# Float64 weights rounded by a 32-bit sum on GpSimd, and all of w_out converted in the first expert

## The chip, the core and the metric

The kernel runs on one core of one Trainium2 chip. The metric is the device time of one execution in microseconds (us). A core has five engines that run at the same time, each through its own instructions in the order in which they were issued: TensorE (PE, matrix products; its weight loads are PEld), VectorE (DVE), ScalarE (ACT), GpSimd (POOL) and SyncE (SP), which here issues most of the DMA transfers. An engine waits on a semaphore where its next instruction needs another engine's result, and everything queued behind that instruction waits as well.

## What is computed

Three steps follow one another. The inputs of the last, `w_in` and `w_out`, are float64, since float32 draws are multiplied by a float64 factor.

```python
# 1. retention: 4 batches x 768 steps, 8 heads of 64
state = gamma * state + einsum('bhd,bhe->bhde', k[t], v[t])
y[t] = scale * einsum('bhd,bhde->bhe', q[t], state)
# 2. x = y as 3072 tokens of 512; 8 experts with room for 384 tokens each
logits = x @ w_gate                 # filled in descending order of the logits,
out[mask_e] = relu(x[mask_e] @ w1[e]) @ w2[e]     # a token goes to one expert
# 3. for every token, with w_in (512 x 2048) and w_out (2048 x 512)
h = x @ w_in
g = maximum(h, 0) + log1p(exp(-abs(h)))
return g @ w_out
```

## The kernel before, in words

**Attention stage.** `Attn.emit` walks over 24 chunks of 128 tokens (4 batches of 6). For chunk j the loop issues the load of `qk` for chunk j+3 and the store of chunk j-2's rows `xs` to DRAM (`xd`), the scores `pA` of chunk j+1 on PE and their masked copy `at` on DVE (L126), the projection `pX` of chunk j-1 (its rows leave through ACT as `xs`, L168, its logits through DVE, L173), the outputs `pY` of chunk j (L138, L142) and the state `pS` (L155). ACT also copies `yT` and `sb` and scales `vh` (L114). POOL scales `qs` (L106, a product of two tiles). Every chunk's PSUM tile has one buffer, so PE's next `pA` waits for `at`, and its next `pX` for `xs` and the logits. After every sixth chunk `R.first_part` runs the first selection step of the routing on DVE.

**Float64 conversion.** Class `Conv` turns float64 words into float32. A piece of 128 x 512 (or 128 x 256) values arrives as pairs of 32-bit words, `raw[:, :, 0]` the low and `raw[:, :, 1]` the high one. `Conv.size` takes the magnitude of the high word on ACT (L240) and its maximum with a smallest value on POOL (L241). The generator `Conv.run` then does the rest on DVE, one instruction to each step; each `yield` ends a step. A `w_in` piece gives two tiles, a rounded part `wih` and a remainder `wil`: six DVE instructions (L255, L257, L260, L266, L268, L270) and a copy on ACT (L262). A `w_out` piece gives one float32 tile with five (L272, L274, L276, L281, L283). `side(j, part)` is called three times in each chunk and brings the generator to `(3 j - 2 + part) * 112 // 69` steps, so that the 16 `w_in` pieces and the first three `w_out` pieces (`kept = 3`) are spread over the attention stage.

**First routing.** `Route.phase` finds the next expert's 384 tokens by counting against thresholds: DVE compares (`G`, L409), PE counts (L416), DVE decides (L466), PE sums (L472), DVE goes on (L476, L456). This runs once before the first expert, with `fill` placing two conversion steps behind a comparison four times (8 steps in all), and once for every further expert, beside the matmuls of the expert before. In the first expert one step of routing follows every group of matmuls, later one follows every second group.

**Experts.** `Ffn.plan` lists groups of matmuls: `m1` and `m2` (x by `w1`, h by `w2`), then `f1` (by `w_in`, L669 to L672) and `f2` (by `w_out`, L767 to L772). A product of float32 is made of three matmuls of split operands (`split_w`: rounded half on ACT, L646, remainder on DVE, L647; `split_act`, `split_g` the same for activations). In the first expert (`i == 0`, from the fourth group on) `Ffn.emit` issues four or three steps of the conversion `F.late` behind every group: 26 pieces of 128 x 256, the other 13 blocks of `w_out`. `split_w` of a `w_out` block first runs the generator until that block is made.

Of the kernel before, what the change touches and what calls it, by code (L numbers as in the profile page):

```python
# [53 lines left out]
class Attn:  # L54
# [166 lines left out]
class Conv:  # L221
    def __init__(self, tc, ctx, W, plan, bufs=3, lead=1):
        self.nc, self.W, self.plan, self.bufs, self.lead = tc.nc, W, plan, bufs, lead
# [13 lines left out]
    def size(self, p):  # L237
        raw = self.raw.pop(p)
        A = self.st.tile([128, self.W], I32, name="cA", bufs=2 * self.lead)
        self.nc.scalar.activation(A.bitcast(FT), raw[:, :, 1].bitcast(FT), AF.Abs)  # L240
        self.nc.gpsimd.tensor_scalar(A.bitcast(FT), A.bitcast(FT), LEAST, None, op0=OP.max)  # L241
        return A, raw[:, :, 0].bitcast(U32), raw[:, :, 1]

    def run(self):
        nc, v, N = self.nc, self.nc.vector, len(self.plan)
        T = lambda name: self.st.tile([128, self.W], I32, name=name, bufs=2)
        self.ahead(0)
        ready = [self.size(q) for q in range(self.lead)]
        for p in range(N):
            self.ahead(p + 1)  # L250
            A, w0, w1 = ready.pop(0)
            X, to = T("cX"), self.plan[p][1]
            if len(to) == 2:
                f = lambda t: t.rearrange("p (a n) -> p a n", a=4)
                v.tensor_scalar(X, A, 3, 0x3ffff000, op0=OP.logical_shift_left, op1=OP.bitwise_and)  # L255
                yield
                v.scalar_tensor_tensor(X, w1, UPPER, X, op0=OP.bitwise_and, op1=OP.bitwise_or)  # L257
                yield
                C = T("cC")
                v.tensor_scalar(C, A, 0x1ff, 3, op0=OP.bitwise_and, op1=OP.logical_shift_left)  # L260
                yield
                nc.scalar.activation(to[0], f(X.bitcast(FT)), AF.Copy)  # L262
                if p + self.lead < N:
                    ready.append(self.size(p + self.lead))
                U = A.bitcast(FT)
                v.scalar_tensor_tensor(U, w0, 2.0 ** -29, C, op0=OP.mult, op1=OP.add)  # L266
                yield
                v.tensor_scalar(C, X, -0x800000, None, op0=OP.bitwise_and)  # L268
                yield
                v.scalar_tensor_tensor(to[1], f(U), 2.0 ** -23, f(C.bitcast(FT)), op0=OP.mult, op1=OP.mult)  # L270
            else:
                v.tensor_scalar(X, A, 3, 0x3fffffff, op0=OP.logical_shift_left, op1=OP.bitwise_and)  # L272
                yield
                v.scalar_tensor_tensor(X, w1, UPPER, X, op0=OP.bitwise_and, op1=OP.bitwise_or)  # L274
                yield
                v.tensor_scalar(A, X, -0x800000, None, op0=OP.bitwise_and)  # L276
                yield
                if p + self.lead < N:
                    ready.append(self.size(p + self.lead))
                e = A.bitcast(FT)  # L280
                v.scalar_tensor_tensor(e, w0, 2.0 ** -52, e, op0=OP.mult, op1=OP.mult)  # L281
                yield
                v.tensor_tensor(to[0], X.bitcast(FT), e, op=OP.add)  # L283
            self.made += 1
            yield

    def step(self, to=None):

        while to is None or self.ops < to:
            self.ops += 1  # L290
            if next(self.gen, self) is self or to is None:
                return
# [11 lines left out]
class Route:  # L304
# [3 lines left out]
    def __init__(self, tc, cp, wp, psum_tile, L, NCH, E):  # L308
        nc = self.nc = tc.nc
        self.tc, self.L, self.N, self.E, self.wp, self.psum_tile = tc, L, NCH, E, wp, psum_tile  # L310
# [6 lines left out]
        for st in (1, 33, 47):  # L317
            self.stc[st] = t([128, 46], FT, f"st{st}")
# [7 lines left out]
        d = t([128, 128], FT, "diff")  # L326
# [8 lines left out]
        r48 = t([48, 24], FT, "r48")  # L335
        it(r48, pattern=[[1, 24]], base=24, channel_multiplier=-1, **imp)
        c48 = t([48, 1], FT, "c48")
# [11 lines left out]
        cid = t([128, N, 2], FT, "cid")  # L349
# [75 lines left out]
    def phase(self, i, slow=True, hum=lambda n: None, fill=lambda l: None):  # L425
# [13 lines left out]
        for l, (J, s1, sh, span) in enumerate(() if last else LEVELS):  # L439
# [9 lines left out]
            for st in (s1, 1):  # L449
# [26 lines left out]
                v.scalar_tensor_tensor(sc[:, :J], ps[:, 64:64 + J], 0.0, self.stc[st][:, :J],  # L476
# [130 lines left out]
class Ffn:  # L607
# [212 lines left out]
    def emit(self):  # L820
# [9 lines left out]
        for n, (fn, i, f, key) in enumerate(G):  # L830
# [6 lines left out]
            if i == 0 and n > 3:  # L837
                for _ in range(4 if n % 3 else 3):
# [66 lines left out]
def model(ctx, tc, qk, kv, w_gate, w1, w2, w_in, w_out, tab, gqt, out, B, H, S):  # L905
# [11 lines left out]
    kept = 3  # L917
    wo = pers.tile([128, kept, 512], FT, name="wo")
    holder = {}
    R = Route(tc, pers, None, lambda: holder["ps"](), L, NCH, E)  # L920
# [24 lines left out]
    wos = [wo[:, f, :] for f in range(kept)] + [wl[:, f, :] for f in range(16 - kept)]  # L945
# [37 lines left out]
```

## Time and profile before

| what | us |
|---|---|
| median of 3 runs (lowest, highest) | 1054.81 (1052.47, 1056.62) |
| the profiled execution, its own time | 1053.3 |
| its span, first to last instruction | 1051.5 |
| PE busy | 995.6 (95%) |
| DVE busy | 685.6 (65%) |
| ACT busy | 565.8 (54%) |
| POOL busy | 135.1 (13%) |

The busy time is the union of an engine's instructions. The shares of the whole span hide that the stages differ: attention takes about the first 134 us, the first routing goes to about 164, the first expert's groups to about 302, and the other seven follow. A rows section below has the stretches that matter.

### The profile page before, as it was taken

How to read it: one execution, taken by the hardware profiler on the slowest of the kernel's cores; microseconds unless marked ns; L12 is line 12 of the kernel's file. 1: busy time of each engine (PE TensorE's matmuls, PEld its weight loads, DVE VectorE, ACT ScalarE, POOL GpSimd, SP SyncE). 2: the span in 40 equal slices, each digit the busy share in tenths (PEclk: the TensorE clock that was granted, in tenths of full speed). 3: DMA queues.
4: the chain of work that ended last, by engine and by line, in shares of the span. 5: the costliest groups of instructions: out<-in, count | busy, mean ns of one | idle time of the engine just before them, and what ended most of it. 6: DMA issues, size and time to landing. Idle time of an engine off the chain costs nothing.

```text
span 1051.5 us, 19105 instructions
## 1 busy us (share of the span) xinstructions
PE 995.6 (95%) x7266; PEld 901.3 (86%) x7266; DVE 685.6 (65%) x1778; ACT 565.8 (54%) x1194; POOL 135.1 (13%) x153
## 2 busy tenths in 40 slices
PE   5998878888899999999999999999999999999997
PEld 5887658877799889999899889888989899999996
DVE  3989977989856756665566566656665744344442
ACT  4877613455544664366536653665356636664654
POOL 3544401212110101010101001100110020001001
PEclk9999999999999999999999999999999999999999
DMA  9999524312241203210231014101410150014000
GB/s 359 399 353 333 195 86 126 123 60 71 81 121 31 61 11 98 84 31 1 85 107 31 2 50 141 31 1 38 124 41 1 41 181 21 1 33 129 1 1 31
DMA packets 40748, 97.55 MB, mean 93 GB/s; under 512 B 5328, under 2 KB 5456, under 8 KB 40656
## 3 DMA queue, kind: packets, MB, share of 16 engines
q1 hardware_dynamic: 36000, 83.12, 23.7%
q0 software_dynamic: 3840, 12.59, 3.5%
q8 instruction: 57, 0.93, 0.4%
q10 hardware_dynamic: 816, 0.63, 0.2%
q14 instruction: 35, 0.29, 0.1%
HBM read 83.73 MB, written 12.58 MB: 92 GB/s over the span
## 4 chain that ended last, share of the span: by engine, by line
PE 68%; issue 13%; DVE 12%; DMA 3%; ACT 2%; POOL 1%; SPq 0%; ACTq 0%; POOLq 0%; DVEq 0%
PE h L669 11%; PE h L672 11%; PE h L670 10%; PE acc L767 7%; PE acc L768 7%; PE acc L772 7%; PE acc L661 3%; PE acc L663 3%; PE acc L662 3%; PE rt L416 2%; DMA kv_t<-in_kv_dram 1%; PE pX L164 1%; DVE wlo L647 1%; DMA rx<-in_moe_w_gate_dram 1%; DVE at L126 1%
## 5 line engine op out<-in xcount | busy, mean ns | idle before, releaser
L733 DVE SCALAR_TENSOR_TENSOR gf<-h,sp 128x384 f32<-128x384 f32 x128 | 71.3, 557 | 187.4 <-ACT sp L731 187.3
L669 PE MATMUL h<-x2h,wih 128*128 128x384 f32 x512 | 176.4, 345 | 2.2 <-DVE xl L657 2.2
L670 PE MATMUL h<-x2h,wil 128*128 128x384 f32 x512 | 173.0, 338 | 0.0
L767 PE MATMUL acc<-whi,gh 128*128 128x512 f32 x384 | 154.2, 402 | 0.0
L768 PE MATMUL acc<-wlo,gh 128*128 128x512 f32 x384 | 152.1, 396 | 0.0
L729 ACT ACTIVATE sp<-h 128x384 f32<-128x384 f32 x128 | 62.6, 489 | 147.1 <-PE h L672 138.6
L672 PE MATMUL h<-x2l,wih 128*128 128x384 f32 x512 | 112.9, 340 | 0.9 <-DVE x2l L657 0.7
L772 PE MATMUL acc<-whi,gl 128*128 128x512 f32 x384 | 111.9, 398 | 1.9 <-DVE gl L747 1.9
L653 ACT ACTIVATE h1h<-h 128x384 fp32r<-128x384 f32 x64 | 31.5, 492 | 146.7 <-PE h L672 109.6
L669 PEld LDWEIGHTS h<-x2h,wih 128*128 128x128 f32 x512 | 96.7, 189 | 8.0 <-DVE xl L657 2.4
L670 PEld LDWEIGHTS h<-x2h,wil 128*128 128x128 f32 x512 | 96.7, 189 | 3.5
L672 PEld LDWEIGHTS h<-x2l,wih 128*128 128x128 f32 x512 | 91.3, 189 | 3.6 <-DVE x2l L657 3.6
L646 ACT ACTIVATE whi<-wraw 128x512 fp32r<-128x512 f32 x128 | 76.7, 624 | 28.7 <-DMA wraw<-in_moe_w_dram 26.9
L780 POOL DMA_INDIRECT out_dram<-rows,ix x24 | 25.2, 1052 | 514.7 <-ACT rows L778 511.3
L647 DVE TENSOR_TENSOR wlo<-wraw,whi 128x512 fp32r<-128x512 f32 x128 | 86.6, 691 | 6.6 <-ACT whi L646 6.6
L772 PEld LDWEIGHTS acc<-whi,gl 128*128 128x128 f32 x384 | 72.4, 189 | 19.9 <-DVE gl L747 2.5
L669 PE MATMUL h<-xh,whi 128*128 128x384 f32 x256 | 88.3, 345 | 0.7 <-ACT xh L656 0.7
L661 PE MATMUL acc<-h1h,whi 128*128 128x384 f32 x256 | 88.4, 345 | 0.0
L670 PE MATMUL h<-xh,wlo 128*128 128x384 f32 x256 | 86.2, 337 | 0.0
L663 PE MATMUL acc<-h1l,whi 128*128 128x384 f32 x256 | 86.2, 337 | 0.0
L662 PE MATMUL acc<-h1h,wlo 128*128 128x384 f32 x256 | 86.2, 337 | 0.0
L767 PEld LDWEIGHTS acc<-whi,gh 128*128 128x128 f32 x384 | 72.7, 189 | 14.3 <-ACT sp L730 2.9
(208 smaller groups left out, 1922.8 us busy)
## 6 DMA issues: line engine op xcount, KB each, us to landing
wraw<-in_moe_w_dram SPq DMA_DIRECT2D x128, 256.0 KB, 2.8
qk_t<-in_qk_dram SPq DMA_DIRECT2D x24, 512.0 KB, 8.8
kv_t<-in_kv_dram SPq DMA_DIRECT2D x24, 512.0 KB, 8.2
raw<-in_moe_w_in_dram SPq DMA_DIRECT2D x16, 512.0 KB, 6.5
raw<-in_moe_w_out_dram SPq DMA_DIRECT2D x26, 256.0 KB, 2.6
xd<-xs SPq DMA_DIRECT2D x24, 256.0 KB, 6.9
raw<-in_moe_w_out_dram SPq DMA_DIRECT2D x3, 512.0 KB, 7.4
gqt<-in_gqt_dram SPq DMA_DIRECT2D x5, 256.0 KB, 8.5
```

Of the source, the lines that this page charges most:

```text
L646: nc.scalar.activation(hi, raw, AF.Copy)
L647: nc.vector.tensor_tensor(lo, raw, hi.bitcast(FT), op=OP.subtract)
L661: nc.tensor.matmul(ps, wh, ah, start=start, stop=False)
L662: nc.tensor.matmul(ps, wl, ah, start=False, stop=False)
L663: nc.tensor.matmul(ps, wh, al, start=False, stop=stop)
L669: mm(ps, wh(d), ah[:, d], start=d == 0, stop=False)
L670: mm(ps, wl(d), ah[:, d], start=False, stop=False)
L672: mm(ps, wh(d), al[:, d], start=False, stop=d == 3)
L733: nc.vector.scalar_tensor_tensor(g, ps, 0.0, a, op0=OP.max, op1=OP.add)
L767: nc.tensor.matmul(ps, gh[:, s], wh, start=f == 0, stop=False)
L768: nc.tensor.matmul(ps, gh[:, s], wl, start=False, stop=False)
L772: nc.tensor.matmul(ps, gl[:, s], wh, start=False, stop=f == 15)
```

## The change

A `w_in` or `w_out` piece is now made from a sum of 32-bit whole numbers. `size` also takes the low word, scaled, into a tile `cB` on ACT, two pieces ahead in the attention stage (one ahead later). DVE puts sign and upper bits into `cB` (one instruction), shifts and masks `cA` (one), and POOL adds the two as int32 (L259), which rounds. For `w_out` the sum is the result. For `w_in` ACT copies the sum to `wih`, and DVE subtracts one piece later (`late`) to give `wil`.

The three `w_out` pieces of the attention stage are gone (`kept = 0`): all 16 blocks, 32 half pieces, belong to the first expert's generator. The pace is 50 steps in place of 112 in attention and one or two steps behind a group of the first expert. `xs` has three buffers instead of two. Constants of `Route` that are needed only at the start move to a pool that ends with the attention stage; `st` shrinks to one column and is read as a broadcast.

```diff
-        xs = self.wk.tile([128, 2, 2, 128], FT, name="xs")
+        xs = self.wk.tile([128, 2, 2, 128], FT, name="xs", bufs=3)
...
+        B = self.st.tile([128, self.W], I32, name="cB", bufs=self.keep[1])
         self.nc.scalar.activation(A.bitcast(FT), raw[:, :, 1].bitcast(FT), AF.Abs)
         self.nc.gpsimd.tensor_scalar(A.bitcast(FT), A.bitcast(FT), LEAST, None, op0=OP.max)
-        return A, raw[:, :, 0].bitcast(U32), raw[:, :, 1]
+        self.nc.scalar.activation(B, raw[:, :, 0].bitcast(U32), AF.Copy, scale=2.0 ** -29)
+        return A, B, raw[:, :, 1]
...
+            v.scalar_tensor_tensor(B, w1, UPPER, B, op0=OP.bitwise_and, op1=OP.bitwise_or)
+            yield
+            v.tensor_scalar(A, A, 3, 0x3fffffff, op0=OP.logical_shift_left, op1=OP.bitwise_and)
+            nc.gpsimd.tensor_tensor(F, A, B, op=OP.add)
+            if p + self.lead < N:
+                ready.append(self.size(p + self.lead))
+            yield
+            if late:
+                v.tensor_tensor(late[1][1], late[0], late[1][0].bitcast(FT), op=OP.subtract)
+                yield
+            late = None
             if len(to) == 2:
...
+                late = F.bitcast(FT).rearrange("p (a n) -> p a n", a=4), to
+                nc.scalar.activation(to[0], late[0], AF.Copy)
             self.made += 1
...
             if i == 0 and n > 3:
-                for _ in range(4 if n % 3 else 3):
+                for _ in range(1 + n % 2):
                     self.late.step()
...
-    kept = 3
+    kept = 0
...
-    cuts += [(rows[f], (wo[:, f],)) for f in range(kept)]
-    cv = Conv(tc, c1, 512, cuts, 5, 2)
+    cv = Conv(tc, c1, 512, cuts, 5, 2, (5, 4))
...
-            cv.step((3 * j - 2 + part) * 112 // 69)
+            cv.step((3 * j - 2 + part) * 50 // 69)
```

On DVE in the attention stage, from one `at` to the next but one. In the kernel before:

```order
L126 TENSOR_TENSOR at<-pA,ctab 128x1024
L260 TENSOR_SCALAR cC<-cA 128x512
L266 SCALAR_TENSOR_TENSOR cA<-raw,cC 128x512
L268 TENSOR_SCALAR cC<-cX 128x512
L173 TENSOR_REDUCE L<-pX 128x8
L270 SCALAR_TENSOR_TENSOR wil<-cA,cC 128x4x128
L255 TENSOR_SCALAR cX<-cA 128x512
L126 TENSOR_TENSOR at<-pA,ctab 128x1024
```

and in the changed kernel:

```order
L126 TENSOR_TENSOR at<-pA,ctab 128x1024
L256 SCALAR_TENSOR_TENSOR cB<-raw,cB 128x512
L258 TENSOR_SCALAR cA<-cA 128x512
L173 TENSOR_REDUCE L<-pX 128x8
L126 TENSOR_TENSOR at<-pA,ctab 128x1024
L264 TENSOR_TENSOR wil<-cA,wih 128x4x128
```

Between two `at` there stood five conversion instructions, and now one or two.

On POOL in the attention stage, where `cA` is the magnitude and `qs` the scaled q of a chunk. Before:

```order
L106 TENSOR_TENSOR qs<-qk_t,gqt 128x512
L241 TENSOR_SCALAR cA<-cA 128x512
L106 TENSOR_TENSOR qs<-qk_t,gqt 128x512
L241 TENSOR_SCALAR cA<-cA 128x512
L106 TENSOR_TENSOR qs<-qk_t,gqt 128x512
```

and in the changed kernel:

```order
L106 TENSOR_TENSOR qs<-qk_t,gqt 128x512
L259 TENSOR_TENSOR cA<-cA,cB 128x512
L242 TENSOR_SCALAR cA<-cA 128x512
L106 TENSOR_TENSOR qs<-qk_t,gqt 128x512
L259 TENSOR_TENSOR cA<-cA,cB 128x512
L242 TENSOR_SCALAR cA<-cA 128x512
```

A sum of two tiles now stands ahead of every maximum, and the next chunk's `qs` behind both.

On DVE in the first expert, around one decision of the routing (`ind`, which PE's next sum reads). Before:

```order
L647 TENSOR_TENSOR wlo<-wraw,whi 128x512
L276 TENSOR_SCALAR cA<-cX 128x256
L281 SCALAR_TENSOR_TENSOR cA<-raw,cA 128x256
L283 TENSOR_TENSOR wol<-cX,cA 128x256
L272 TENSOR_SCALAR cX<-cA 128x256
L466 TENSOR_SCALAR ind<-rt,r_113 128x46
```

and in the changed kernel:

```order
L637 TENSOR_TENSOR wlo<-wraw,whi 128x512
L258 TENSOR_SCALAR cA<-cA 128x256
L256 SCALAR_TENSOR_TENSOR cB<-raw,cB 128x256
L456 TENSOR_SCALAR ind<-rt,r_121 128x46
```

Four conversion instructions stood ahead of `ind`; now two do, and the second needs a `cB` that ACT is told to make just ahead of it.

## Rows read from the trace of the kernel before

**Rows 1.** Busy time in stretches: us, then engines, granted clock, DMA share, GB/s.

```profile
27.00:60.00 33.00, 29.69 (x454) 26.09 (x451) 31.03 (x57) 24.62 (x74) 16.75 (x11) 0.95 0.99 380
27.00:131.00 104.00, 90.69 (x1414) 79.34 (x1412) 98.93 (x180) 77.44 (x228) 49.18 (x33) 0.97 0.86 321
175.00:266.00 91.00, 80.37 (x560) 72.58 (x559) 84.80 (x251) 45.71 (x98) 22.68 (x25) 0.98 0.29 89
414.00:489.00 75.00, 75.00 (x486) 69.50 (x485) 48.02 (x140) 39.65 (x77) 6.06 (x7) 1.00 0.20 61
```

In these rows the engines stand in the order PE, PEld, DVE, ACT, POOL.

**Rows 2.** Chain that ended last: start, us, what; chunks 2, 3 and 23.

```profile
27.06 1.02 PE pY L142 x16
31.36 1.02 PE pY L142 x16
...
130.56 1.05 PE pY L142 x16
```

**Rows 3.** Waits of PE, 27 to 134 us: total us, times, longest.

```profile
PE pX L164 <- DVE L L173: 6.1, 5, 1.8
PE pA L125 <- DVE at L126: 5.0, 3, 2.4
```

**Rows 4.** One line's matmuls, first and last start; first expert, then the third.

```profile
L661 PE MATMUL acc<-h1h,whi x32: 333/337/423, 175.2 to 207.8; 128*128 128x384 f32 x32
L767 PE MATMUL acc<-whi,gh x48: 391/396/632, 220.3 to 300.8; 128*128 128x512 f32 x48
...
L661 PE MATMUL acc<-h1h,whi x32: 334/337/423, 414.1 to 443.5; 128*128 128x384 f32 x32
L767 PE MATMUL acc<-whi,gh x48: 391/396/478, 450.6 to 519.0; 128*128 128x512 f32 x48
```

**Rows 5.** Waits of PE in the first expert, 175 to 292 us.

```profile
PE rt L472 <- DVE ind L466: 7.2, 6, 2.9
PE rt L526 <- DVE tb L523: 2.3, 1, 2.3
```

**Rows 6.** Three lines of DVE: ns min/median/max, first and last start.

```profile
L255 DVE TENSOR_SCALAR cX<-cA x16: 410/421/1539, 19.8 to 114.8; 128x512 int32<-128x512 int32 x16
...
L257 DVE SCALAR_TENSOR_TENSOR cX<-raw,cX x16: 675/692/1726, 20.6 to 115.3; 128x512 int32<-128x512 int32 x16
...
L647 DVE TENSOR_TENSOR wlo<-wraw,whi x128: 671/685/917, 159.7 to 968.6; 128x512 fp32r<-128x512 f32 x128
```

**Rows 7.** The longest L257 and what POOL ran then: start, us.

```profile
57.27 1.27 POOL L106 TENSOR_TENSOR qs<-qk_t,gqt 128x512 f32<-128x512 f32 x1 [0.54 <-DVE wil L270]
...
57.36 1.73 DVE L257 SCALAR_TENSOR_TENSOR cX<-raw,cX 128x512 int32<-128x512 int32 x1
```

**Rows 8.** Groups by shape, start to 330 us: busy us, mean ns, idle before.

```profile
L241 POOL TENSOR_SCALAR cA<-cA 128x512 f32<-128x512 f32 x19 | 30.5, 1608 | 52.4 <-ACT cA L240 51.3 <-PE pS L155 1.1
L106 POOL TENSOR_TENSOR qs<-qk_t,gqt 128x512 f32<-128x512 f32 x20 | 27.3, 1366 | 14.2 <-DMA qk_t<-in_qk_dram 11.2 <-PE pY L138 1.8 <-DVE cC L260 0.6
L241 POOL TENSOR_SCALAR cA<-cA 128x256 f32<-128x256 f32 x26 | 23.6, 909 | 94.6 <-ACT cA L240 94.6
L168 ACT ACTIVATE xs<-pX 128x512 f32<-128x512 f32 x24 | 14.2, 592 | 14.8 <-DMA xd<-xs 6.9 <-PE pX L164 4.3 <-issue 3.3
L274 DVE SCALAR_TENSOR_TENSOR cX<-raw,cX 128x256 int32<-128x256 int32 x26 | 11.3, 434 | 0.6
L240 ACT ACTIVATE cA<-raw 128x512 f32<-128x512 f32 x19 | 12.7, 676 | 0.0
L240 ACT ACTIVATE cA<-raw 128x256 f32<-128x256 f32 x26 | 11.2, 429 | 27.5 <-DVE wol L283 23.5 <-DVE thr L456 3.9
```

**Rows 9.** One group by shape on DVE, 134 to 300 us.

```profile
L272 DVE TENSOR_SCALAR cX<-cA 128x256 int32<-128x256 int32 x26 | 7.4, 286 | 0.0
```

**Rows 10.** DVE in the first routing, start and us.

```profile
142.72 0.24 DVE L469 TENSOR_SCALAR thrA<-jio,zero 128x46 f32<-128x46 f32 x1
...
143.61 0.80 DVE L409 TENSOR_TENSOR G<-kx,thr 128x552 bf16<-128x552 f16 x2
```

More of the change, by code (lines that the diff above doesn't have):

```diff
@@ L221, with __init__ @@
 class Conv:
-    def __init__(self, tc, ctx, W, plan, bufs=3, lead=1):
-        self.nc, self.W, self.plan, self.bufs, self.lead = tc.nc, W, plan, bufs, lead
+    def __init__(self, tc, ctx, W, plan, bufs=3, lead=1, keep=(3, 2)):
+        self.nc, self.W, self.plan, self.bufs, self.lead, self.keep = tc.nc, W, plan, bufs, lead, keep
         self.st = ctx.enter_context(tc.tile_pool(name="cst", bufs=2, side="right"))
@@ L238, in size @@
         raw = self.raw.pop(p)
-        A = self.st.tile([128, self.W], I32, name="cA", bufs=2 * self.lead)
+        A = self.st.tile([128, self.W], I32, name="cA", bufs=self.keep[0])
+        B = self.st.tile([128, self.W], I32, name="cB", bufs=self.keep[1])
         self.nc.scalar.activation(A.bitcast(FT), raw[:, :, 1].bitcast(FT), AF.Abs)
         self.nc.gpsimd.tensor_scalar(A.bitcast(FT), A.bitcast(FT), LEAST, None, op0=OP.max)
-        return A, raw[:, :, 0].bitcast(U32), raw[:, :, 1]
+        self.nc.scalar.activation(B, raw[:, :, 0].bitcast(U32), AF.Copy, scale=2.0 ** -29)
@@ L244, in run @@
+        return A, B, raw[:, :, 1]
     def run(self):
         nc, v, N = self.nc, self.nc.vector, len(self.plan)
-        T = lambda name: self.st.tile([128, self.W], I32, name=name, bufs=2)
         self.ahead(0)
         ready = [self.size(q) for q in range(self.lead)]
+        late = None
         for p in range(N):
             self.ahead(p + 1)
-            A, w0, w1 = ready.pop(0)
-            X, to = T("cX"), self.plan[p][1]
-            if len(to) == 2:
[L254 to L283, printed above, removed]
@@ new lines, in run @@
+            A, B, w1 = ready.pop(0)
+            to = self.plan[p][1]
+            F = to[0].bitcast(I32) if len(to) == 1 else A
+            v.scalar_tensor_tensor(B, w1, UPPER, B, op0=OP.bitwise_and, op1=OP.bitwise_or)
[5 more added lines that the diff above has]
+            yield
@@ L284, in run @@
+            if late:
+                v.tensor_tensor(late[1][1], late[0], late[1][0].bitcast(FT), op=OP.subtract)
+                yield
+            late = None
+            if len(to) == 2:
+                late = F.bitcast(FT).rearrange("p (a n) -> p a n", a=4), to
+                nc.scalar.activation(to[0], late[0], AF.Copy)
             self.made += 1
-            yield
+        if late:
+            v.tensor_tensor(late[1][1], late[0], late[1][0].bitcast(FT), op=OP.subtract)
+        while True:
+            yield self
@@ L290, in step @@
             self.ops += 1
-            if next(self.gen, self) is self or to is None:
+            if next(self.gen) is self or to is None:
                 return
@@ L304, with __init__ @@
 class Route:
-    def __init__(self, tc, cp, wp, psum_tile, L, NCH, E):
+    def __init__(self, tc, cp, tp, wp, psum_tile, L, NCH, E):
         nc = self.nc = tc.nc
+        x = lambda shape, dt, name: tp.tile(shape, dt, name=name)
         self.tc, self.L, self.N, self.E, self.wp, self.psum_tile = tc, L, NCH, E, wp, psum_tile
@@ L334, in __init__ @@
         v.tensor_scalar(self.u48[0:24, 0:24], d[0:24, 0:24], 0.0, None, op0=OP.is_gt)
-        r48 = t([48, 24], FT, "r48")
+        r48 = x([48, 24], FT, "r48")
         it(r48, pattern=[[1, 24]], base=24, channel_multiplier=-1, **imp)
-        c48 = t([48, 1], FT, "c48")
+        c48 = x([48, 1], FT, "c48")
         it(c48, pattern=[[0, 1]], base=0, channel_multiplier=1, **imp)
@@ L925, in model @@
     rows = [w_out[f * 128:(f + 1) * 128] for f in range(16)]
-    cuts += [(rows[f], (wo[:, f],)) for f in range(kept)]
-    cv = Conv(tc, c1, 512, cuts, 5, 2)
+    cv = Conv(tc, c1, 512, cuts, 5, 2, (5, 4))
+    init = c2.enter_context(tc.tile_pool(name="rinit", bufs=1, side="right"))
+    R = Route(tc, pers, init, None, lambda: holder["ps"](), L, NCH, E)
     a = Attn(tc, c2, aps, qk, kv, w_gate, tab, gqt, ident, L, xd, B, H, S)
@@ L944, in model @@
     wl = late.tile([128, 16 - kept, 512], FT, name="wol")
-    wos = [wo[:, f, :] for f in range(kept)] + [wl[:, f, :] for f in range(16 - kept)]
+    wos = [wl[:, f, :] for f in range(16)]
     R.wp = ctx.enter_context(tc.tile_pool(name="rwork", bufs=1, reuse_waits="tile"))
```

10 lines of the change are left out of this document (4 added, 6 removed).

## The prediction

> **What bounds the kernel now.** I read the stretches first, then the chain, then PE's waits in the two stages that the change touches. Over the whole span PE is busy 95%, and the last seven experts leave nothing to win: between 414 and 489 us PE is busy 75.0 of 75 us [rows 1]. The conversion runs in attention and in the first expert, and there the engine that is full is DVE: 98.9 of 104 us between 27 and 131, and 84.8 of 91 between 175 and 266 [rows 1]. In attention the chain shows chunk 2's `pY` at 27.06 and chunk 3's at 31.36, so PE can do a chunk in 4.30 us; from chunk 3 to chunk 23 it took (130.56 - 31.36) / 20 = 4.96 us for each [rows 2]. PE was idle for 104 - 90.7 = 13.3 us of that stretch, and 11.1 us of waits name two DVE instructions, the logits and `at` [rows 1, 3]. DMA is the neighbour: its share was 0.99 at 380 GB/s while loads ran [rows 1]. In the first expert the stretch from the first `m2` matmul to the last `f2` took 300.8 - 175.2 = 125.6 us, and the same groups of the third expert 519.0 - 414.1 = 104.9 us [rows 4]: 20.7 us more for the same products. PE's waits there name DVE too, most of them a decision of the routing (7.2 and 2.3 us) [rows 5].
>
> **Attention, term by term.** DVE loses per `w_in` piece six instructions: three like L255 (median 0.42 us; L260 and L268 have the same shape) and three like L257 (0.69; L266 and L270) [rows 6], 3.33 us. It gets one like L257, one like L255 and a subtraction like L647 (0.69) [rows 6], 1.80 us. That is 16 x 1.53 = 24.5 us less. The three `w_out` pieces go with five instructions each, 2 x 0.42 + 3 x 0.69 = 2.91, or 8.7 us. Together 33.2 us are taken from DVE.
>
> What is added is a POOL sum of two tiles, 16 times, and here the trace has a warning. While POOL ran the product L106 from 57.27 to 58.54, an L257 that started at 57.36 took 1.73 us instead of 0.69, ending 0.55 us after the product [rows 6, 7]: it stood still until POOL was done. Yet POOL was busy for 49.2 of 104 us, much of it with the maximum L241, and the medians of rows 6 lie within 3% of the minima, so most instructions are not held up, and POOL's one-input work seldom holds any [rows 1, 6]. The new sum has no row. The nearest is L106, a product of two 128 x 512 tiles at 1.37 us [rows 8]; a whole-number sum may cost more or less. Its effect on DVE lies between nothing and its full length, 16 x 1.37 = 21.9 us. I take half, 11 us. DVE's load is then 98.9 - 33.2 + 11 = 76.7 in a stretch of some 97 us, and it stops being the bound.
>
> The Trainium skill, "SBUF — State Buffer", section "Who interferes with whom", says that a VectorE instruction with two SBUF inputs and a GpSimd instruction that reads SBUF exclude each other, and that the one that began keeps the shared port to its end. The L257 above agrees; by that rule at its fullest every sum holds DVE for its length, DVE's load in this stretch would be 87.6 us, and the gain there would shrink to some 4 us.
>
> What is late next? ACT: 16 more instructions like L240 (0.68) and three fewer make 8.8 us on top of 77.4, 86.2 of some 97 us [rows 1, 8], tight but below PE. The copy to `wih` now waits for POOL's sum, and behind it in ACT's queue stand `yT`, `sb` and `xs`, for which PE waits; the copy is issued two steps, nearly a chunk, behind the sum, which hides 1.37 us and the 1.61 us of a maximum ahead of it. POOL gets 16 x 1.37 - 3 x 1.61 = 17.1 us, 66.3 of 97, and `qs` stands behind it, two chunks ahead of its use. DMA: a chunk moves 1 MB of `qk` and `kv`, 0.26 of `xs` and, at 50 steps in place of 112, 0.73 of a 0.52 MB piece in place of 0.81; with `gqt` some 1.7 MB, at 380 GB/s 4.45 us [rows 1]. The third `xs` buffer costs nothing and takes away up to 6.9 us in which ACT waited for stores [rows 8].
>
> So PE's floor is 4.30 us per chunk, DMA's 4.45, and I add 0.15 for ACT's load and the bursts of `first_part`: 4.60. That gives 20 x (4.96 - 4.60) = **7 us gained**. The ends: 13 us (the floor, all of PE's idle time) and 2 us lost (ACT held by late sums).
>
> **The first routing.** Each of the four fills had two DVE instructions, and now has an L257-like and an L255-like one of half the size, the same 0.43 + 0.29 us [rows 8, 9]. Behind them POOL runs the sum (1.37 x 909 / 1608 = 0.77 us, by the ratio of the maximum's two sizes [rows 8]) and the next maximum, while DVE comes to `thrA` and `G` [rows 10], on the path of the decision. Each fill may lose nothing or up to 0.6 us: 0 to 2.4, I take **1 us lost**.
>
> **The first expert.** The 26 half pieces cost 3 x 0.43 + 2 x 0.29 = 1.87 us each [rows 8, 9]; 8 of their 130 steps lie in the routing, so 24.4 x 1.87 = 45.6 us lie here. Now 32 pieces cost 0.72; four lie in the routing, and 28 x 0.72 = 20.2 us here. The 28 sums hold DVE between 0 and 28 x 0.77 = 21.6 us; half is 10.8. Net 45.6 - 20.2 - 10.8 = 14.6 us less on DVE, and 84.8 becomes 70.2, below the 75 us that PE needs for the same groups in the third expert [rows 1]. PE then sets the pace except at the routing's decisions, which still come a group after their count: some of the waits of rows 5 stay. ACT gets 28 x 2 - 24.4 instructions of 0.43 us, 13.6 on top of 45.7 [rows 1, 8], with room. DVE's L256 now waits for `cB`, which in every other piece ACT makes just ahead; two ACT instructions, 0.86 us, against the `h1l` or `gf` and L258 that DVE does meanwhile. SP issues 32 loads of 256 KB in place of 26 here (DMA share 0.29 [rows 1]), and the conversion is always ahead of `until`: it makes 16 pieces by the time the block of `f = 4` needs 10. I take **11 us gained** of the 20.7; the ends are 4 (sums hold DVE to the full) and 17. The remaining experts keep their work.
>
> **Sum.** 7 - 1 + 11 = 17 us, from the profiled execution's 1053.3 to 1036.3. The median of the three runs lies 1.5 us above that execution, so I forecast 1037.5.
>
> **Rivals.** *ACT takes DVE's place in attention.* For it: 86 of 97 us and a copy that waits for POOL. Against: it has nearly a chunk of slack. The gain there is nil: 1053.3 + 1 - 11 = 1043, for the median 1045. *The routing keeps PE waiting in the first expert.* For it: 9.5 us of rows 5 are decisions that follow a chain of PE, DVE and ACT, and DVE now also waits for `cB`; the lock held to the full gives the same. Only 4 us are gained: 1053.3 - 7 + 1 - 4 = 1043, median 1045. *Both stages reach PE's floor.* 13 and 16 us gained, nothing lost: 1024, median 1026. *The whole-number sum is slow, and DVE stands behind it: slower.* It holds DVE to its end; the savings of 33.2 and 25.4 us are used up when a sum takes 33.2 / 16 = 2.1 us in attention and 25.4 / 28 = 0.9 us here. At twice L106 (2.74 and 1.54 us) DVE gets 10.6 and 17.7 us more than before in stages that it bounded: 1053 + 28 = 1081; at one and a half times, with the stages as they were in attention, 32.3 - 25.4 = 7 us more here, 1060. The trace has no whole-number instruction on POOL to say how likely. *It doesn't do what it says*: `until` would have to run the conversion in bursts, which the counts above exclude.
>
> The Trainium skill, "GPSIMD Engine Reference", section "When to use GPSIMD", keeps element by element work on VectorE, since a two-input instruction is about half as fast on GpSimd. Rows 6 and 8 agree (1.37 against 0.69 us); by that rule alone the change would be a loss, which is the slow sum's case and has its chance.
>
> **How the numbers follow.** Forecast 0.46 (1030 to 1041), ACT 0.15, routing 0.18, both at the floor 0.14, slow sum 0.06, not as said 0.01. The predicted time is the likeliest, 1037.5. From 1027 to 1048 the range takes in the forecast, both rivals at 1045 and the upper part of the floor case, and leaves out the rest of it and the slow sum. A measurement tells about 0.5%, 5.3 us, from no change: faster means below 1049.5. All cases but the slow sum and the last lie below, less some spread of those at 1045: faster 0.88, same 0.06, slower 0.06.
>
> **What would show it.** In the changed profile: `pY` of chunk 23 near 123 us; DVE busy some 80% between 27 and the end of attention; PE's waits on the logits and `at` down from 11.1 us to a few; the sum L259 near 1.4 and 0.8 us, and DVE instructions stretched beside it; in the first expert `m2` to the last `f2` about 115 us instead of 125.6. It is wrong if the sum takes over 2 us, if ACT's waits on POOL at the copy to `wih` come to more than a few us, or if PE's waits on `ind` stay at 7 us or grow.

## The result, and the profile after

The changed kernel takes **1038.2 us** (median of four executions, 1036.8 to 1039.7) where the kernel before took 1054.0 in the same session: a ratio of **0.985 (0.982 to 0.988)**. The forecast was 1037.5, within 1027 to 1048. The profiled span fell from 1051.5 to 1037.6 us, 13.9 us less. By stage, from the starts of the same matmuls:

| stage | before | after | difference | forecast |
|---|---|---|---|---|
| start to `pY` of chunk 23 | 130.5 us | 124.8 | -5.7 | -7 |
| to the first `m2` of expert 1 | 44.7 | 47.9 | +3.2 | +1 |
| to the last `f2` of expert 1 | 125.6 | 113.4 | -12.2 | -11 |
| sum | 300.8 | 286.1 | -14.7 | -17 |

These rows answer to rows of before. First the two stretches of [rows 1], engines in the same order:

```profile
27.00:125.00 98.00, 90.92 (x1420) 79.71 (x1418) 69.16 (x123) 82.81 (x239) 63.45 (x45) 0.96 0.86 325
172.00:253.00 81.00, 78.72 (x565) 72.20 (x564) 69.06 (x192) 53.90 (x122) 42.45 (x45) 1.00 0.35 109
```

DVE was busy 98.9 of 104 us in attention and is now busy 69.2 of 98. It no longer bounds that stage. In the first expert PE is busy 78.7 of 81 us where it was 80.4 of 91.

The chain of work that ended last answers to [rows 2] (start, length, what):

```profile
27.88 1.13 PE pY L142 x16
...
85.00 1.58 PE pY L142 x16
89.85 1.02 PE pY L142 x16
94.16 1.02 PE pY L142 x16
98.46 1.02 PE pY L142 x16
...
101.70 1.02 PE pY L142 x16
...
124.88 1.05 PE pY L142 x16
```

Chunks 15 to 17 follow each other at 4.30 us, PE's own pace, and chunk 18, the first of a batch, comes 3.24 us after chunk 17: the last chunk of a batch has no `pS`, and the first no product with the state (L138). What is left over sits in a few places, the largest in this list ahead of 85.00 (chunk 14). PE's waits between 27 and 128 us answer to [rows 3] and those between 172 and 290 us to [rows 5] (total us, times, longest):

```profile
PE pA L125 <- DVE at L126: 5.8, 3, 3.6
PE pX L164 <- ACT yT L145: 1.5, 3, 0.8
PE pX L164 <- ACT sb L157: 0.5, 1, 0.5
...
PE h L659 <- DVE xl L647: 2.0, 1, 2.0
PE rt L462 <- DVE ind L456: 1.5, 1, 1.5
PE acc L762 <- DVE gl L737: 0.8, 1, 0.8
PE rt L516 <- DVE tb L513: 0.7, 1, 0.7
```

The waits on the logits (6.1 us) are gone. Those on `at` are not. In the expert the waits on `ind` and `tb` fell from 9.5 to 2.2 us.

The sum's price, which no row of before showed, by shape from the start to 330 us (busy us, mean ns, idle before), with the ACT instructions around it:

```profile
L259 POOL TENSOR_TENSOR wol<-cA,cB 128x256 int32<-128x256 int32 x32 | 28.5, 889 | 63.1 <-DVE cA L258 39.3 <-ACT whi L636 19.7 <-DVE ik L391 2.3
L259 POOL TENSOR_TENSOR cA<-cA,cB 128x512 int32<-128x512 int32 x16 | 21.6, 1353 | 24.4 <-DVE cA L258 24.4
...
L243 ACT ACTIVATE cB<-raw 128x256 int32<-128x256 uint32 x32 | 13.7, 429 | 17.4 <-POOL wol L259 17.4
L269 ACT ACTIVATE wih<-cA 128x512 fp32r<-128x512 f32 x16 | 10.1, 628 | 0.1
```

The whole-number sum takes 1.35 and 0.89 us, next to 1.37 and 0.77 assumed. ACT's copy to `wih` waited 0.1 us in all, so the rival in which ACT takes DVE's place has no support. ACT does stand behind the sums in the first expert, 17.4 us at L243, where the next low word needs one of only two `cB` tiles.

### The profile page after: what moved, and what is told of

Same layout as the page of the kernel before. It is cut to its first block, busy times and chain, and to the rows that moved or that the text cites. A ratio compares the mean times of both kernels' runs of the same rounds, so it can differ in the third digit from the quotient of the medians.

```text
span 1037.6 us, 19094 instructions
## 1 busy us (share of the span) xinstructions
PE 994.5 (96%) x7266; PEld 901.9 (87%) x7266; DVE 636.3 (61%) x1649; ACT 585.0 (56%) x1245; POOL 186.1 (18%) x204
## 4 chain that ended last, share of the span: by engine, by line
PE 72%; issue 12%; POOL 5%; DVE 5%; DMA 2%; ACT 2%; another core or an unknown queue 0%; SPq 0%; ACTq 0%; POOLq 0%
PE h L659 11%; PE h L662 11%; PE h L660 10%; PE acc L757 7%; PE acc L762 7%; PE acc L758 7%; PE acc L651 3%; PE acc L653 3%; PE acc L652 3%; PE pX L164 2%; POOL wol L259 2%; PE pA L125 2%; POOL cA L242 2%; PE pY L142 2%; PE rt L406 2%
## 5 line engine op out<-in xcount | busy, mean ns | idle before, releaser
L762 PE MATMUL acc<-whi,gl 128*128 128x512 f32 x384 | 111.2, 396 | 0.8 <-DVE gl L737 0.8
L637 DVE TENSOR_TENSOR wlo<-wraw,whi 128x512 fp32r<-128x512 f32 x128 | 86.3, 689 | 6.1 <-ACT whi L636 6.1
L637 DVE TENSOR_TENSOR wlo<-wol,whi 128x512 fp32r<-128x512 f32 x128 | 89.0, 698 | 0.9 <-ACT whi L636 0.9
L636 ACT ACTIVATE whi<-wraw 128x512 fp32r<-128x512 f32 x128 | 76.6, 624 | 17.1 <-DMA wraw<-in_moe_w_dram 14.2
```

Of the source, the lines that this page charges most:

```text
L636: nc.scalar.activation(hi, raw, AF.Copy)
L637: nc.vector.tensor_tensor(lo, raw, hi.bitcast(FT), op=OP.subtract)
L762: nc.tensor.matmul(ps, gl[:, s], wh, start=False, stop=f == 15)
```

## The experiments

Ratios are to the kernel before, run beside each on the same chip. The last three columns are of one profiled execution each: `pY` of chunk 0 to chunk 23, from there to the first `m2`, and from there to the last `f2` of the first expert.

| kernel | median us | ratio (95%) | attention | routing | expert 1 |
|---|---|---|---|---|---|
| before | 1054.0 | 1 | 118.1 | 44.7 | 125.6 |
| changed | 1038.2 | 0.985 (0.982-0.988) | 112.6 | 47.9 | 113.4 |
| new in the expert alone, 26 halves | 1040.2 | 0.986 (0.982-0.989) | 118.9 | 48.9 | 108.9 |
| new in attention alone, 3 pieces of `w_out` there | 1044.5 | 0.990 (0.988-0.993) | 106.5 | 45.6 | 124.6 |
| new in both, 3 pieces there | 1029.5 | 0.978 (0.976-0.980) | 107.9 | 46.2 | 108.9 |
| one-input op for the sum | 1031.7 | 0.977 (0.975-0.980) | 109.6 | 47.4 | 109.8 |
| each sum twice | 1057.4 | 1.003 (1.001-1.004) | 113.0 | 49.0 | 128.3 |
| first part later | 1031.5 | 0.979 (0.978-0.981) | 107.1 | 46.3 | 112.0 |
| no steps in the routing | 1044.9 | 0.992 (0.991-0.994) | 109.2 | 44.5 | 125.4 |
| the same, two steps per group | 1044.4 | 0.991 (0.988-0.994) | 109.9 | 45.7 | 122.3 |
| two `xs` buffers | 1038.9 | 0.987 (0.985-0.988) | 111.2 | 47.7 | 113.5 |
| routing's step first | 1038.8 | 0.986 (0.983-0.989) | 108.3 | 47.9 | 114.3 |
| 3 pieces and first part later | **1026.7** | 0.975 (0.972-0.977) | 105.2 | 47.1 | 108.9 |
| 6 pieces and first part later | 1036.5 | 0.983 (0.981-0.985) | 115.0 | 47.3 | 108.2 |

Four kernels of this table have the same attention code (changed, no steps, two steps, routing's step first). They took 108.3 to 112.6 us there, 110.0 on average, and differed at chunk 2 (7.8 to 10.2 us) and chunk 14 (8.9 to 10.3). Around chunk 2, from 20 to 28 us, the mean granted clock was 0.58 and 0.79 in two of them and 1.00 in the other two; at chunk 14 it fell in all four. A difference in attention under 4 us between two profiled executions therefore says nothing by itself. The first expert is steadier: 113.4, 113.5 and 114.3 with the same pieces.

### The two halves of the new arithmetic, apart

One kernel keeps the old generator in attention (called `Old` here), the other in the first expert. Both keep the three pieces of `w_out` in attention, as before, and give the old generator its old pace; the first also has two `xs` buffers again.

```diff
...
-    kept = 0
+    kept = 3
...
-    cv = Conv(tc, c1, 512, cuts, 5, 2, (5, 4))
+    cv = Old(tc, c1, 512, cuts, 5, 2)
...
```

```diff
...
-    kept = 0
+    kept = 3
...
-    F.late, F.kept = Conv(tc, ctx, 256, halves, 3), kept
+    F.late, F.kept = Old(tc, ctx, 256, halves, 3), kept
...
```

> Attention as in the kernel before (old conversion of w_in and of three w_out blocks, two xs buffers), the new conversion only for the 26 half pieces of the first expert. Theory (the gain is DVE relieved in two stages that do not depend on each other; in the changed kernel chunk 23 came 5.7 us earlier, the stretch from the last chunk to the first m2 took 3.2 us more, and m2 to the last f2 12.2 us less): attention unchanged, the routing stretch 1 to 3 us longer, m2 to the last f2 about 113 us; 1044 to 1046 us. Rival (the first expert gains only because DVE's and the clock's state at its start is better after a shorter attention stage): m2 to the last f2 over 119 us, over 1049 us.

> The new conversion and the third xs buffer in attention, there also for three w_out blocks (57 steps), the old conversion and its pace in the first expert. Theory: chunk 23's pY 4 to 6 us earlier than 130.5, the first expert's m2 to last f2 unchanged at 125 to 126 us; 1047 to 1050 us. Rival (the three w_out blocks moved out make the gain in attention, not the new conversion): chunk 23 at 129 or later, 1052 or more.

Both came out faster than their theories said: 1040.2 and 1044.5 us. In the expert alone the stage fell by 16.7 us, to 108.9, more than the 12.2 of the changed kernel, because 26 half pieces were converted there or in the routing and not 32. In attention alone the stage took 106.5 us, 11.6 less than before and 6 less than the changed kernel (3.5 less than the average of the four above), with three pieces *more* to convert. The prediction had counted the three pieces' 8.7 us on DVE among the savings in attention. By these runs taking them out of that stage gains nothing, so they were put back next.

### Three pieces back in attention

```diff
-    kept = 0
+    kept = 3
...
-            cv.step((3 * j - 2 + part) * 50 // 69)
+            cv.step((3 * j - 2 + part) * 57 // 69)
...
```

> The changed kernel with three pieces of w_out back in the attention, as the kernel before had them, all by the new arithmetic (57 steps over the chunks instead of 50, 26 half pieces in the first expert instead of 32). Theory (the stages stand by themselves, so the attention comes out as in the run with the new arithmetic in the attention alone, pY of chunk 23 near 119, and the first expert as in the run with it in the expert alone, near 109 us from its first m2 to its last f2): median 1027 to 1031. Rival (the routing between them takes it back: its VectorE chain starts earlier but its waits and TensorE's half clock grow, 49 us or more, or the attention's better time was the chance place of one step): median 1033 to 1037.

1029.5 us, as the theory had it. The halves add up: 15.5 us (expert alone) and 11.2 (attention alone) below the 1055.7 measured beside them make 26.7, and the two together gave 24.2. Against 0.985, 0.987 and 0.986 for the changed kernel and its two neutral variants, 0.978 is some 8 us less. **The move of all of `w_out` into the first expert, as issued here, cost about 8 us** out of the 24 that the arithmetic gave. By one profiled execution each, the expert is 4.5 us shorter with three pieces back, a stage that repeats within 1 us. The 1.7 us in the routing are the clock more than the move (see below on the routing). In attention the difference is chunk 14: 6.3 us with 57 steps, in both kernels that have them and the old place of `first_part`, against 8.9 to 10.3 with 50. So a part of the 8 us is which step of the conversion stands beside the routing's burst. With `first_part` moved (below) the same three pieces are worth 5 us.

### The sum: its kind, and its length

One kernel replaces each sum by a maximum of one tile, so that the weights come without sign and upper bits. Another issues each sum twice, the second into `cB`.

```diff
-            nc.gpsimd.tensor_tensor(F, A, B, op=OP.add)
+            nc.gpsimd.tensor_scalar(F.bitcast(FT), A.bitcast(FT), LEAST, None, op0=OP.max)
```

```diff
             nc.gpsimd.tensor_tensor(F, A, B, op=OP.add)
+            nc.gpsimd.tensor_tensor(B, F, B, op=OP.add)
```

> The changed kernel with POOL's sum of two tiles replaced by a maximum of one tile and a constant, of the same size and at the same place, so that the weights lack sign and upper bits. Theory (POOL's two-input sum holds DVE's two-input instructions to its end): DVE instructions beside it are no longer stretched, the routing stretch about 1 us shorter, attention 1 to 3 us shorter, first expert 1 to 3 us shorter; 1033 to 1036 us. Rival (the holding costs nothing, as DVE has room everywhere): 1037 to 1039 us.

> The changed kernel with every POOL sum issued twice (the second into the dead cB). Theory (holding): another 1.3 and 0.8 us of held DVE behind each, partly hidden; routing 1 to 2 us longer, attention 1 to 4, first expert 2 to 5; 1042 to 1049 us. Rival (ACT's copy to wih, which waits for the sum, is the narrow place of attention): attention 8 us or more longer and ACT's waits on POOL at the copy over 5 us; over 1050 us. Rival (DVE has room): under 1041 us.

With the one-input operation the kernel took 1031.7 us, some 8 less by the ratios (0.977 against 0.985). That operation is *longer*; its groups by shape (busy us, mean ns):

```profile
L259 POOL TENSOR_SCALAR wol<-cA 128x256 f32<-128x256 f32 x32 | 32.1, 1004 | 61.8 <-DVE cA L258 58.4 <-DVE ik L391 2.2 <-DVE inc L493 0.4
...
L259 POOL TENSOR_SCALAR cA<-cA 128x512 f32<-128x512 f32 x16 | 25.0, 1562 | 23.4 <-DVE cA L258 18.1 <-DVE L L173 3.1 <-PE pY L142 2.1
```

So POOL's own time does not make the difference. The same 1649 DVE instructions took (first lines of the pages: changed, then one input)

```profile
PE 994.5 (96%) x7266; PEld 901.9 (87%) x7266; DVE 636.3 (61%) x1649; ACT 585.0 (56%) x1245; POOL 186.1 (18%) x204
...
PE 992.2 (96%) x7266; PEld 899.8 (87%) x7266; DVE 628.4 (61%) x1649; ACT 584.2 (57%) x1245; POOL 189.1 (18%) x204
```

7.9 us less; five other runs with as many DVE instructions and the sum of two tiles lie between 634.1 and 640.2. Counted in the changed kernel's trace, 68 DVE instructions started beside a running sum; 28 of them were held (over 0.15 us longer than the shortest of their line and shape), by 13.7 us in all. While POOL ran the one-input maximum L242, 96 started and 16 were held, by 3.8 us. Of the reductions (L173 and the like) that started beside one of these two or the product L106, 0 of 22 were held.

This run does not settle that DVE alone makes the 8 us. The maximum does not read `cB`, so the wait of ACT's low words for a sum, 17.4 us in the changed kernel, is gone as well:

```profile
L243 ACT ACTIVATE cB<-raw 128x256 int32<-128x256 uint32 x32 | 13.5, 423 | 3.0 <-DVE cB L256 3.0
```

By stage, the expert is 3.6 us shorter, and attention (109.6) is no shorter than in the four kernels above.

With each sum twice the time was 1057.4, past the theory's 1049: its rival's verdict, but not its mechanism. Attention hardly changed (113.0) though POOL was busy 91 of 98 us there. The expert lost 14.9 us. The rows between 165 and 305 us:

```profile
ACT cB L243 <- POOL cB L260: 32.8, 17, 5.8
...
DVE cA L258 <- POOL cA L242: 18.1, 16, 3.2
```

DVE waited for POOL's maximum (7.8 us in the changed kernel), which stood behind both sums, and ACT for `cB`. At the copy to `wih`, where the rival had looked, ACT waited 3.0 us in attention. There DVE's busy time rose too, from 69.2 to 80.2 of 98 us, and the stage hid it; in the expert it was not hidden. Pieces are prepared two ahead in attention and one ahead in the expert, which fits, but no run varied this by itself.

### The burst of the routing in attention

Ahead of `pY` of chunk 14 the changed kernel's timeline shows (start, length, engine, what, idle before):

```profile
72.40 1.27 POOL L259 TENSOR_TENSOR cA<-cA,cB 128x512 int32<-128x512 int32 x1 [0.96 <-DVE cA L258]
72.69 1.05 DVE L384 TENSOR_TENSOR lm<-L,m 128x48 f32<-128x48 f32 x1
...
75.09 2.50 POOL L106 TENSOR_TENSOR qs<-qk_t,gqt 128x512 f32<-128x512 f32 x2
75.18 1.20 DVE L394 SCALAR_TENSOR_TENSOR kf<-sg,unas 128x6 f32<-128x6 int32 x1
76.42 1.20 DVE L395 TENSOR_SCALAR kx<-kf 128x12 f16<-128x12 f32 x1
...
78.48 1.22 DVE L126 TENSOR_TENSOR at<-pA,ctab 128x1024 f32<-128x1024 f32 x1
79.75 2.08 PE L125 MATMUL pA<-qk_t 64*128 64x128 f32 x16 [3.59 <-DVE at L126]
```

`first_part` issues small DVE instructions, some of 6 or 12 columns, that otherwise take about 0.2 us. Three of them stood until a two-input POOL instruction ended, and `at`, queued behind them, kept PE idle for 3.59 us. PE then ran at half clock: the 16 matmuls of `pA` took 2.08 us, otherwise 1.16. The experiment moves `first_part` one chunk later and behind the next `at`:

```diff
             if j + 1 < n:
                 self.qk(j + 1)
+            if j > 1:
+                logits(j - 2)
             side(j, 0)
...
-            if j:
-                logits(j - 1)
             side(j, 2)
+        logits(n - 2)
```

> One change to the changed kernel: the first part of the routing's calculation for a batch (the burst of some sixteen small VectorE instructions after chunks 5, 11, 17, 23) is issued one chunk later and behind that chunk's A*cos/sin product instead of ahead of it. Theory (the burst, lengthened by GpSimd's sums and products that run beside it, stands ahead of the product for which TensorE waits, 3.6 us at chunk 14, and TensorE's clock then falls to half for some 7 us): chunk 13 to 14 falls from 10.3 us to between 4.3 and 6, chunk 19 to 20 from 5.9 to under 5, pY of chunk 23 begins near 119 instead of 124.8, the median near 1032 to 1034. Rival (the burst is not what sets chunk 14, or its wait is met again one step on): pY of chunk 23 stays at 123.5 to 126 and the median at 1037 to 1040.

1031.5 us, below the theory's range, with `pY` of chunk 23 at 119.8. PE's waits between 20 and 128 us:

```profile
PE pA L125 <- DMA qk_t<-in_qk_dram: 3.6, 1, 3.6
PE pX L164 <- DVE L L173: 2.5, 1, 2.5
```

No wait on `at` is left. Chunk 14 came down only to 8.3 us, not to 6, since the burst now stands ahead of `L` (2.5 us). The other row is a wait for a load of `qk_t`. The kernel without steps in the routing, which has the changed kernel's attention, shows a wait of 3.4 us for `qk_t` too. The medians differ by 6 to 7 us; by one profiled execution, attention is 3 us below the average of the four kernels with the same steps, and the rest is spread over routing and expert.

### The steps in the first routing, and the lead they give

```diff
-            for _ in range(2 if level else 0):
+            for _ in range(0):
```

and, in a second kernel, also

```diff
-                for _ in range(1 + n % 2):
+                for _ in range(2):
```

> The changed kernel without the steps of conversion inside the first routing (some four half pieces that then go to the first expert). Theory (GpSimd's sums hold VectorE's chain in the routing, about 2 of the 3.2 us by which it grew): from pY of chunk 23 to the first m2 47.8 falls to 45 to 46, the first expert grows from 113.4 to 115 to 117, median 1037 to 1040. Rival (the steps there cost nothing, the growth is TensorE's half clock alone): the routing stays at 47 to 48.5, the first expert grows by the same 2 to 4, median 1040 to 1043.

> The kernel without steps of conversion in the first routing, but with two steps behind each group of the first expert instead of one or two by turns. Theory (without the head start the pieces came just when the split of w_out on ScalarE needed them, ScalarE stood behind GpSimd's sums for 14 us and the first expert took 125.4 us; it is the lead that was missing, not VectorE's time): first expert 113 to 117, median 1033 to 1037. Rival (the four pieces more are too much work for VectorE in the first expert wherever they stand): first expert 120 or more, median 1040 or more.

Without these steps the routing took 44.5 us in the first kernel, as before the change (44.7), and 45.7 in the second, whose code is the same up to the expert. What differs between these two is PE's clock: six filler matmuls (L869, whose result nothing reads) behind the routing's second decision ran at either level. First the kernel without steps, then the one with two steps per group, then the one with three pieces in attention, which has the steps:

```profile
130.86 1.62 PE L869 MATMUL pA<-wih 128*128 128x512 f32 x6
...
131.81 2.91 PE L869 MATMUL pA<-wih 128*128 128x512 f32 x6
...
129.63 1.63 PE L869 MATMUL pA<-wih 128*128 128x512 f32 x6
```

From 4 to 8 us behind `pY` of chunk 23 PE was busy for 2.4 us in each of the first two; in the next 4 us the mean granted clock was 1.00 in the first and 0.50 in the second. The third kernel had the full clock through the whole routing, and took 46.2 us there. So the steps cost some 1.5 us, next to the forecast's 1, and the changed kernel, where the six took 2.91 us too, lost the other half of its 3.2 while the clock was low. But without the steps the expert went from 113.4 to 125.4 us, far past the 115 to 117 expected. ACT's waits between 215 and 260 us name a new one:

```profile
ACT whi L636 <- POOL wol L259: 11.1, 6, 2.5
ACT cB L243 <- POOL wol L259: 7.3, 6, 2.2
```

The split of `w_out` itself (L636) stood behind sums not yet done. My next theory was that only the lead was missing. Two steps behind each group restored it: each row of `w_out` was then ready 23 to 34 us ahead of its `f2`, in place of 8 to 28. The expert still took 122.3 us, so **that theory fell**. ACT's first two waits in that kernel, 168 to 300 us, and PE's first two:

```profile
ACT cB L243 <- POOL wol L259: 16.2, 15, 2.8
ACT h1h L643 <- PE h L662: 12.5, 8, 3.5
...
PE rt L462 <- DVE ind L456: 4.4, 5, 1.5
PE rt L510 <- DVE mem L507: 2.3, 1, 2.3
```

The denser steps delay the routing's decisions instead. By the number of half pieces converted in the expert, it took 108.2 us with 16, 108.9 with 22, 113.4 with 28 and 122.3 or 125.4 with 32: nothing up to 22, about 0.75 us for each of the next six, 2 to 3 us for each of the last four. (With these four came a shorter lead in one kernel and denser steps in the other, so their price is not that of the number alone.) Whether ACT or DVE sets that edge is not settled. A third `cB` tile, against ACT's wait at L243, was not tried.

### Two parts without effect

```diff
-        xs = self.wk.tile([128, 2, 2, 128], FT, name="xs", bufs=3)
+        xs = self.wk.tile([128, 2, 2, 128], FT, name="xs")
```

```diff
-            if i == 0 and n > 3:
-                for _ in range(1 + n % 2):
-                    self.late.step()
             step += 1
             if self.listed <= i + 1 or step % 2 == 0:
                 self.route()
+            if i == 0 and n > 3:
+                for _ in range(1 + n % 2):
+                    self.late.step()
```

> The changed kernel with two buffers for xs, as before, instead of three: this part of the change undone. Theory (no wait of the path rests on it): pY of chunk 23 within 1.5 us of 124.8 and the median 1037 to 1040. Rival (the third buffer, by which ScalarE no longer waits for the stores of xs, carries part of the attention's gain): pY of chunk 23 at 127 to 129, median 1041 to 1043.

> The changed kernel with the conversion's steps of the first expert issued behind the next expert's routing step of the same group instead of ahead of it. Theory (TensorE still waits 5 us in the first expert for results of the routing and of the first layer on VectorE, which stand behind the conversion): first expert 111 to 113 instead of 113.4, median 1035.5 to 1038. Rival (the steps come later against the split of w_out that needs them, whose lead is short): first expert 114.5 or more, median 1039 or more.

The third `xs` buffer carries nothing (1038.9 us). Issuing the routing's step first gave 1038.8, just outside both statements, and 114.3 in the expert: no gain that can be told.

### Together, and one step further

> Both changes that were faster by themselves: three pieces of w_out back in the attention, and the first part of the routing's calculation behind the next chunk's product. Theory (each takes away what it took away alone; of the 5.5 us for which TensorE waited for the product in the run with three pieces some 3.5 go, the wait for the load of qk_t at chunk 14 stays): pY of chunk 23 begins near 117, the first expert lasts 109, median 1025 to 1027. Rival (in the attention the loads are the floor until some 84 us, their share of the 16 DMA engines being full, so what the product gives back the wait for qk_t takes): pY of chunk 23 at 119 to 121, median 1028 to 1030.

> The fastest version so far (three pieces of w_out in the attention, the first part of the routing's calculation behind the next product) with six pieces in the attention instead of three: 63 steps over the chunks instead of 57, 20 half pieces after it instead of 26. Theory (in the attention a piece costs nothing as long as TensorE has VectorE's and GpSimd's results in time, as three more pieces cost nothing before; in the first expert the last six half pieces still cost 2 to 4 us, its excess over the third expert being 4.1): pY of chunk 23 within 1.5 us of 117.7, first expert 105.5 to 107.5, median 1023 to 1026. Rival (the attention is full: three more loads of 512 KB on DMA engines that are full until some 84 us, and VectorE and GpSimd near 80%, put TensorE behind): pY of chunk 23 at 120 or more, median 1027 or more.

Three pieces with the later `first_part` gave **1026.7 us**, 11.5 below the changed kernel: `pY` of chunk 23 at 117.7 and the expert at 108.9, as the theory said. The two gains do not add up in full, since both shorten chunk 14 (10.3 us in the changed kernel, 6.3 and 8.3 with either, 5.9 with both): the pieces are worth 5 us here and not 8, the later burst some 3 and not 6. PE's first three waits in attention were

```profile
PE pA L125 <- DMA qk_t<-in_qk_dram: 4.0, 2, 3.3
PE pX L164 <- ACT vh L114: 2.5, 2, 1.6
PE pX L164 <- DVE L L173: 1.6, 1, 1.6
```

DVE's are the smallest. With six pieces the rival held: 1036.5 us and `pY` of chunk 23 at 127.7. Its waits in attention:

```profile
PE pX L164 <- DVE L L173: 5.1, 2, 3.6
PE pX L164 <- ACT vh L114: 2.9, 1, 2.9
PE pA L125 <- DVE cB L257: 2.1, 1, 2.1
```

The expert gained 0.7 us where 1.4 to 3.4 were expected, and attention lost 10. The best place for the pieces lies between none and six.

## Why the prediction was right, and where it was not

**The bound.** That DVE bounded attention and the first expert held: DVE's page total fell from 685.6 to 636.3 us and both stages shortened. The signals came as named, but for DVE's load in attention (71%, not some 80%) and `at`. The forecast's last step has a slip, far inside the scatter: 1036.3 and 1.5 make 1037.8, not 1037.5.

**Attention, -7 forecast, -5.7 seen, -8 on average over four profiled executions of the same code.** The size was right and two terms in it were not. First, half of each sum's length was taken as DVE's loss, 21.8 us over both stages. Replacing the sums gave DVE back 7.9, and counting instructions that started beside a sum gives 13.7. The term was too large. Second, the 0.15 us per chunk for ACT and the bursts, 3 us over 20 chunks, was too small at one place: chunk 14 alone took 10.3 us, where a two-input POOL instruction held the burst. [rows 7] had shown the mechanism. The prediction applied it to the conversion's large instructions and not to small ones that stand ahead of `at`. A DVE that is busy 71% still kept PE waiting, because its delay came in one piece. That these 20 chunks took 4.63 us each where 4.60 were forecast is in part luck: the floor was taken as 4.45, DMA's, for all of them, while nine took 4.30, the three that begin a batch 3.24 and the last 3.80. That is some 5.6 us less, and it made up for what the burst's term lacked.

The Trainium skill, "SBUF — State Buffer", section "Who interferes with whom", says that the shared port is an exclusive lock and that a VectorE reduction on this chip never contends for it. The changed kernel's trace agrees on the reductions, held 0 of 22 times, and on two-input POOL instructions. By the page a one-input GpSimd maximum, which reads SBUF, should hold a two-input VectorE instruction to its end as well; here 20 large ones (L256, L264, L637, L737) started beside a maximum, 15 took their usual time and five 0.2 to 0.3 us longer.

**The routing, +1 forecast, +3.2 seen.** What the sum left out is PE's clock. The fills cost some 1.5 us, by the kernel that has them at full clock (46.2), inside the 0 to 2.4 that the prediction gave them; 0.9 us of DVE instructions held beside the sums is part of that. The rest came with half clock: six filler matmuls took 2.91 us instead of 1.64, which is 0.9 us on the way to the next decisions, and from 164 to 168 us the mean granted clock was 0.58. The first is no price of the fills, since of the two kernels without them one had it and one did not. Whether the second is, stays open: of the kernels with fills some had it and some did not. One of each in the changed kernel's timeline (`thrA`, L459, takes 0.24 us in [rows 10]):

```profile
133.97 2.91 PE L869 MATMUL pA<-wih 128*128 128x512 f32 x6
...
143.60 0.73 POOL L259 TENSOR_TENSOR wol<-cA,cB 128x256 int32<-128x256 int32 x1 [1.84 <-DVE cA L258]
143.73 0.64 DVE L459 TENSOR_SCALAR thrA<-jio,zero 128x32 f32<-128x32 f32 x1
```

**The first expert, -11 forecast, -12.2 seen.** Right in size. DVE's net relief was put at 14.6 us and 11 of them taken. But the sum counted in one figure a gain of 16.7 us (expert alone) and a loss of 4.5 for six more half pieces, which it priced by DVE's 0.72 us each on an engine that would have room. That is about what they cost, 0.75, up to 28 pieces, and a third of what the next four cost.

**What the sum hid.** The change has two parts of opposite sign: arithmetic worth 24 us and a move worth -8 (-5 where the burst stands later). The prediction saw "three pieces fewer" in attention as 8.7 us off DVE, in a stage where DVE was about to stop being the bound. Relieving an engine that another part had already freed was worth nothing here, and the same pieces cost time where they went.

**The rivals.** ACT in DVE's place: refuted at the copy (0.1 us). Routing keeps PE waiting: `ind` and `tb` fell to 2.2 us. Both at the floor: nearly reached by the best version, 1026.7 us. The slow sum: at twice its length the kernel took 1057.4, 0.3% slower than before, so slower as that rival said, but by 3 us and not 27, since in attention the second sum is hidden.

## What to carry to other kernels

Price each part of a change against the state that the other parts leave, and test the parts apart: a total that is right may hold a loss that can be undone (here 5 to 8 us). When work goes from a full engine to one that shares something with it, look less at the busy shares than at the short instructions that stand just ahead of what the main engine waits for; moving a burst behind them was worth 6 us in the changed kernel and 3 in the better one, without taking any work away. Moved work was nearly free up to an edge here and dear behind it, so measure two or three amounts. And look at PE's clock before a few us in one stage are put down to a change.

## What the runs showed of the hardware

- A 32-bit whole-number sum of two 128x512 tiles on POOL takes 1.35 us on average, a float product of that shape 1.39 in the same trace. A one-input maximum takes 1.53 to 1.56 us, longer than either, and yet holds DVE far less: of 20 large two-input DVE instructions that started beside it none waited for its end. Beside a sum 12 of 19 did; of the others four started within its last 0.11 us, and three beside two sums that were themselves delayed.
- Small instructions are held like large ones: one of 6 columns (L394), otherwise some 0.2 us, took 1.20 us beside the product.
- After PE had been idle for 3.59 us its next 16 matmuls of `pA` took 2.08 us instead of 1.16, and a stretch from 76 to 84 us shows a mean granted clock of 0.70, a mix of the two levels 1.2 and 2.4 GHz. The same instructions ran at either level from one kernel to the next: the six fillers above, 1.62 and 2.91 us. The stretch:

```profile
76.00:84.00 8.00, 4.41 (x34) 3.79 (x34) 6.48 (x10) 4.33 (x15) 4.31 (x4) 0.70 0.99 370
```
